# RWKV attention into a SwiGLU FFN: grouping the FFN by batches at the start, with a new order of all steps

## The chip, the cores and the metric

The kernel runs on one core of a Trainium2 chip. The metric is the device time of one execution in microseconds. A core has five instruction queues that run independently: TensorE (PE: matmuls, transposes by matmul, and its weight loads, PEld), VectorE (DVE), ScalarE (ACT), GpSimd (POOL) and SyncE (SP, which issues most transfers). Each runs its own instructions in order and waits on semaphores for the others. Matmuls write to PSUM, eight banks of 2 KB per partition; everything else lies in SBUF or in HBM.

## The reference

Four batches, 8 heads, 768 time steps, head width 48. A linear recurrence with decay w feeds an RMS norm and a gated FFN (384 to 1536 to 384):

```
for t in range(S):
    cur = einsum('bhd,bhe->bhde', u * k_t, v_t)
    y_t = einsum('bhd,bhde->bhe', r_t, state + cur)
    state = w_t[..., None] * state + einsum('bhd,bhe->bhde', k_t, v_t)
x  = y as (B*S, 384)
xn = x / sqrt(mean(x*x) + 1e-6) * rms_g
out = (silu(xn @ w_gate) * (xn @ w_val)) @ w_out
```

## The kernel before

The 768 steps are cut into 6 chunks of 128 (n = 0 to 5). A unit is one chunk of one batch (j = 0 to 3), so there are 24 attention units, and a batch's chunk n + 1 needs the state of its chunk n. The FFN runs once per chunk, over the four batches' 4 x 128 = 512 tokens: 12 blocks f of 128 hidden features.

The order of all work is written out by hand in ORDER (L25 to L128), a list of steps `name.n.j`; the loop at L691 calls the function of that name, which appends instructions to the engines' queues. So the place of a step in ORDER is its place in each queue it uses.

For an attention unit the steps are: load_w, load_r, load_k, load_v (SP; in chunks 0 and 1 one load_w brings both chunks of a batch); ln (ACT, log of w); cs_mm (PE, cumulative sums), cs_add (DVE, chunks 2 to 5); exp_r and exp_k (ACT); r_mul (DVE) and k_mul (DVE or POOL, by K_POOL); w_tot (DVE); rk_pe with rk_tr (PE transposes and a copy out of PSUM, chunks 0 and 1) or rk_tr alone (a transposing transfer); q_mm (PE), q_mask_e (DVE), q_copy_o (ACT) with q_mask_o (POOL), or q_mask_o on DVE; bonus_mul (POOL: r times k, then times u), bonus_sum (DVE), bonus_v (POOL); cast_v (ACT or POOL, by CAST_ACT); y_mm (PE); st_mm (PE) and st_new (DVE) for the state; x_pe (PE) or x_add (DVE); x_sq (ACT), x_rstd (ACT or POOL, by RSTD_ACT), xn_mul (ACT); xn_pe with xn_out (PE, DVE), or xn_tr with xn_gain (transfer, then DVE or ACT) in the last two chunks.

For the FFN of a chunk: gate_mm and val_mm (PE, three matmuls each, fc_mm at L626), silu (ACT), h_mul (DVE, L658) for each f, then o_mm (PE, twelve matmuls, L672), o_out (DVE or ACT, by OUT_DVE) and out_dma (SP) for each batch. The last o_mm is split into two halves of 192 columns.

PSUM is handed out by psum() from three rings: "a" (two banks: gate, cumulative sums, some y), "b" (two banks: val, cumulative sums, some y) and "q" (four banks: the rest). act() loads ScalarE's table at L233 whenever a step needs Exp or Ln behind Silu or the reverse. The FFN weights come by load_gv(g, h) and load_wo(g) on POOL's queue, cast from fp32 to bf16 on the way; gate and val are cut at f = 0, 4, 12, so there are four such loads of unequal size, and three for w_out. 13 dummy matmuls at L285 and 36 warm steps (L374) on zeros keep PE busy at the start.

The kernel's text with its line numbers, cut to what the change touches:

Of the kernel before, what the change touches and what calls it, by code (L numbers as in the profile page):

```python
# [25 lines left out]
load_w.0.1 load_r.0.0 load_w.0.0 warm.4.0 warm.18.0 load_r.0.1 load_k.0.1 load_w.0.2 load_k.0.0 ln.0.1 load_k.0.2  # L26
load_w.0.3 ln.0.0 load_r.0.2 warm.31.0 load_v.0.0 load_v.0.1 warm.22.0 load_k.0.3 load_r.0.3 load_v.0.3 load_v.0.2
cs_mm.0.1 exp_r.0.1 exp_k.0.1 cs_mm.0.0 load_r.1.1 load_k.1.0 load_r.1.0 load_k.1.1 w_tot.0.1 ln.0.2 warm.10.0
load_r.1.3 load_k.1.3 load_r.1.2 load_k.1.2 r_mul.0.1 load_v.1.0 load_v.1.2 load_v.1.1 exp_k.0.0 bonus_mul.0.1
load_v.1.3 load_w.2.0 warm.7.0 exp_r.0.0 k_mul.0.1 bonus_mul.0.0 rk_pe.0.1 w_tot.0.0 warm.2.0 warm.21.0 load_w.2.1  # L30
rk_tr.0.1 warm.9.0 cs_mm.0.2 warm.27.0 bonus_sum.0.1 exp_r.0.2 r_mul.0.0 k_mul.0.0 bonus_mul.0.2 warm.12.0 warm.34.0
warm.13.0 ln.0.3 r_mul.0.2 warm.26.0 rk_pe.0.0 exp_k.0.2 warm.5.0 rk_tr.0.0 load_r.2.1 load_w.2.2 warm.19.0 warm.32.0
cast_v.0.0 cs_mm.0.3 load_r.2.0 load_k.2.0 q_mm.0.1 warm.8.0 w_tot.0.2 k_mul.0.2 bonus_sum.0.0 exp_k.0.3 cs_mm.1.0
bonus_v.0.1 q_mm.0.0 exp_r.0.3 exp_k.1.0 q_mask_e.0.1 q_mask_o.0.1 bonus_sum.0.2 k_mul.0.3 exp_r.1.0 w_tot.0.3
r_mul.0.3 warm.24.0 warm.29.0 rk_pe.0.2 warm.1.0 x_pe.0.1 cast_v.0.1 rk_tr.0.2 y_mm.0.1 bonus_v.0.0 bonus_mul.0.3
q_mask_o.0.0 rk_pe.0.3 q_mask_e.0.0 q_mm.0.2 x_pe.0.0 x_sq.0.1 cast_v.0.3 rk_tr.0.3 bonus_sum.0.3 q_mask_o.0.2
load_gv.0.0 q_mask_e.0.2 cs_mm.1.1 x_rstd.0.1 q_mm.0.3 warm.17.0 bonus_v.0.2 q_mask_o.0.3 y_mm.0.0 warm.25.0 exp_r.1.1
load_w.2.3 x_pe.0.2 load_k.2.1 cast_v.0.2 bonus_v.0.3 warm.20.0 x_sq.0.0 y_mm.0.2 st_mm.0.0 warm.6.0 warm.35.0
xn_mul.0.1 x_rstd.0.0 x_sq.0.2 warm.15.0 q_mask_e.0.3 warm.23.0 x_pe.0.3 xn_mul.0.0 warm.3.0 warm.16.0 y_mm.0.3
exp_k.1.1 cs_mm.1.3 k_mul.1.0 xn_pe.0.1 warm.0.0 bonus_mul.1.0 load_gv.0.1 load_gv.1.0 x_rstd.0.2 warm.30.0 x_sq.0.3  # L40
xn_mul.0.2 r_mul.1.0 st_new.0.0 xn_pe.0.0 warm.14.0 x_rstd.0.3 warm.28.0 warm.33.0 xn_pe.0.2 xn_out.0.1 bonus_mul.1.1
warm.11.0 xn_mul.0.3 exp_k.1.3 xn_out.0.0 st_mm.0.3 xn_out.0.2 st_mm.0.2 xn_pe.0.3 exp_r.1.3 cs_mm.1.2 xn_out.0.3
r_mul.1.1 st_new.0.3 k_mul.1.1 k_mul.1.3 gate_mm.0.0 exp_r.1.2 bonus_sum.1.0 exp_k.1.2 gate_mm.0.3 st_mm.0.1
st_new.0.1 rk_pe.1.0 val_mm.0.0 rk_pe.1.1 silu.0.0 rk_tr.1.0 bonus_sum.1.1 load_gv.1.1 load_r.2.2 bonus_mul.1.3
silu.0.3 val_mm.0.2 rk_tr.1.1 h_mul.0.0 gate_mm.0.2 st_new.0.2 silu.0.2 gate_mm.0.1 bonus_sum.1.3 val_mm.0.3
gate_mm.0.9 silu.0.1 h_mul.0.2 val_mm.0.1 gate_mm.0.6 silu.0.9 r_mul.1.3 h_mul.0.3 q_mm.1.0 h_mul.0.1 silu.0.6
q_mask_e.1.0 q_copy_o.1.0 q_mask_o.1.0 gate_mm.0.11 gate_mm.0.7 q_copy_o.1.1 silu.0.7 rk_pe.1.3 q_mask_e.1.1
q_mask_o.1.1 r_mul.1.2 bonus_v.1.0 val_mm.0.6 val_mm.0.7 k_mul.1.2 rk_tr.1.3 cast_v.1.0 gate_mm.0.5 h_mul.0.6 y_mm.1.0
load_wo.0.0 val_mm.0.9 silu.0.11 bonus_v.1.1 cast_v.1.2 load_wo.1.0 st_mm.1.0 cast_v.1.1 gate_mm.0.4 rk_pe.1.2
h_mul.0.7 st_mm.1.1 silu.0.5 val_mm.0.5 x_add.1.0 rk_tr.1.2 h_mul.0.9 cast_v.1.3 gate_mm.0.10 bonus_mul.1.2 val_mm.0.4  # L50
st_new.1.0 st_new.1.1 load_wo.2.0 q_mm.1.2 h_mul.0.5 silu.0.4 x_sq.1.0 h_mul.0.4 gate_mm.0.8 bonus_v.1.3 q_copy_o.1.3
x_rstd.1.0 q_mask_e.1.3 q_copy_o.1.2 val_mm.0.8 silu.0.8 val_mm.0.11 y_mm.1.1 silu.0.10 q_mask_e.1.2 bonus_sum.1.2
q_mask_o.1.3 h_mul.0.8 x_add.1.1 y_mm.1.3 st_mm.1.2 load_v.2.1 ln.2.0 st_mm.1.3 q_mask_o.1.2 val_mm.0.10 y_mm.1.2
x_sq.1.1 xn_mul.1.0 bonus_v.1.2 cs_mm.2.0 x_add.1.3 x_sq.1.3 st_new.1.2 h_mul.0.11 ln.2.1 h_mul.0.10 x_add.1.2
cs_add.2.0 o_mm.0.0 o_out.0.0 x_rstd.1.1 x_sq.1.2 xn_pe.1.0 xn_out.1.0 xn_mul.1.1 exp_r.2.0 st_new.1.3 cs_mm.2.1
cs_add.2.1 x_rstd.1.2 load_r.2.3 r_mul.2.0 o_mm.0.2 xn_pe.1.1 xn_mul.1.2 xn_pe.1.2 x_rstd.1.3 o_mm.0.1 xn_mul.1.3
bonus_mul.2.0 xn_out.1.1 exp_k.2.0 out_dma.0.0 load_k.2.2 exp_r.2.1 w_tot.2.0 load_v.2.0 ln.2.2 k_mul.2.0 ln.2.3
w_tot.2.1 r_mul.2.1 cs_mm.2.2 xn_pe.1.3 cs_mm.2.3 exp_k.2.1 xn_out.1.2 cs_add.2.2 k_mul.2.1 cs_add.2.3 cast_v.2.1
exp_r.2.2 exp_r.2.3 rk_tr.2.1 xn_out.1.3 o_mm.0.3 exp_k.2.3 o_out.0.1 w_tot.2.2 r_mul.2.2 bonus_mul.2.1 gate_mm.1.7
val_mm.1.7 exp_k.2.2 load_k.2.3 st_mm.2.1 rk_tr.2.0 bonus_sum.2.0 r_mul.2.3 w_tot.2.3 gate_mm.1.1 load_v.2.2  # L60
# [664 lines left out]
```

## Time and profile before

| quantity | value |
|---|---|
| median of 3 runs | 200.59 us (200.36 to 200.87) |
| span of the profiled execution | 199.6 us |
| busy in that span: PE, DVE, ACT, POOL | 192.4, 151.6, 137.5, 125.0 us |
| weight loads (PEld) | 113.9 us |
| granted TensorE clock, mean | 0.999 |
| HBM read, written | 25.96 MB, 4.72 MB |

The profiled execution's span reaches from its first to its last instruction. Rows of the profile name a line of the kernel, the engine, the operation, output <- input by the program's names, the shape, and a count; then busy time, the mean of one in ns, and the idle time of the engine just before such instructions with what ended it. PE's busy time counts the dummy matmuls too, and the ends of matmuls are modelled, so that start to start is the better measure of one.

### The profile page before, as it was taken

What the parts mean: (1) busy time and instruction counts of PE and PEld (TensorE: products, weight loads), DVE (VectorE), ACT (ScalarE), POOL (GpSimd) and SP (SyncE); (2) the same over time, 40 slices, a digit from 0 to 9 for tenths busy, and PEclk for the clock granted to TensorE, in tenths of its full rate; (3) what the DMA queues carried; (4) which work ended last, traced back from release to release, by engine and by line L of the source; (5) the groups of instructions that cost most, each with busy time, mean ns of one, the idle gap of its engine ahead of it and who ended that gap; (6) DMA issues with size and microseconds to landing.
All of it is one profiled execution on the core that took longest, in us unless ns stands there. A gap on an engine that the chain in (4) does not pass through costs nothing.

```text
span 199.6 us, 4410 instructions
## 1 busy us (share of the span) xinstructions
PE 192.4 (96%) x1577; PEld 113.9 (57%) x1577; DVE 151.6 (76%) x290; ACT 137.5 (69%) x279; POOL 125.0 (63%) x184
## 2 busy tenths in 40 slices
...
GB/s 148 249 230 174 184 194 204 201 207 198 156 180 233 181 158 235 226 205 204 208 213 220 211 197 207 171 176 148 116 181 232 1 23 61 0 118 82 0 59 100
DMA packets 121566, 32.41 MB, mean 162 GB/s; under 512 B 116420, under 2 KB 120392, under 8 KB 121544
## 3 DMA queue, kind: packets, MB, share of 16 engines
...
q0 software_dynamic: 2032, 3.54, 10.1%
q8 instruction: 12, 0.20, 0.4%
q14 instruction: 10, 0.08, 0.1%
...
HBM read 25.96 MB, written 4.72 MB: 154 GB/s over the span
## 4 chain that ended last, share of the span: by engine, by line
PE 71%; SPq 13%; DMA 11%; POOL 2%; issue 1%; ACT 0%; POOLq 0%
SPq L248 11%; PE ps_av L626 10%; PE ps_bu L626 10%; PE ps_bv L626 10%; PE ps_au L626 9%; DMA vt<-in_v_dram 7%; PE ps_qz L672 7%; PE ps_qv L672 7%; PE ps_qu L672 5%; PE ps_qx L672 4%; DMA wo_sb<-in_moe_w_out_dram 4%; SPq L261 2%; PE ps_qv L502 1%; PE ps_qx L552 1%; PE ps_av L417 1%
## 5 line engine op out<-in xcount | busy, mean ns | idle before, releaser
L672 PEld LDWEIGHTS <-ht 128*128 128x128 bf16 x300 | 28.2, 98 | 17.3 <-issue 0.7
L626 PEld LDWEIGHTS <-wg_sb 128*128 128x128 bf16 x216 | 23.1, 114 | 20.2 <-DMA wg_sb<-in_moe_w_gate_dram 0.7
L626 PEld LDWEIGHTS <-wv_sb 128*128 128x128 bf16 x216 | 22.8, 114 | 18.6 <-DMA wv_sb<-in_moe_w_val_dram 0.5
L658 DVE TENSOR_TENSOR ht<-ps_bv,sg 128x512 bf16<-128x512 f32 x35 | 24.0, 686 | 10.1 <-PE ps_bv L626 9.2
L235 ACT ACTIVATE sg<-ps_av 128x512 bf16<-128x512 f32 x37 | 22.0, 595 | 12.3 <-PE ps_av L626 12.1
L626 PE MATMUL ps_av<-xnt,wg_sb 128*128 128x512 bf16 x111 | 30.1, 380 | 0.0
L626 PE MATMUL ps_bu<-xnt,wv_sb 128*128 128x512 bf16 x111 | 30.1, 380 | 0.0
L658 DVE TENSOR_TENSOR ht<-ps_bu,sg 128x512 bf16<-128x512 f32 x37 | 25.4, 686 | 6.0 <-PE ps_bu L626 5.2
L467 POOL TENSOR_TENSOR ruk<-rt,kt 128x384 f32<-128x384 f32 x24 | 24.0, 1002 | 8.7 <-DVE wcol L446 4.5
L626 PE MATMUL ps_bv<-xnt,wv_sb 128*128 128x512 bf16 x105 | 28.5, 380 | 0.3 <-DMA wv_sb<-in_moe_w_val_dram 0.3
L626 PE MATMUL ps_au<-xnt,wg_sb 128*128 128x512 bf16 x105 | 28.5, 380 | 0.3 <-DMA wg_sb<-in_moe_w_gate_dram 0.2
L235 ACT ACTIVATE sg<-ps_au 128x512 bf16<-128x512 f32 x35 | 21.0, 599 | 10.8 <-PE ps_au L626 9.0
L468 POOL TENSOR_TENSOR ruk<-ruk,u_bc 128x384 f32<-128x384 f32 x24 | 24.4, 1017 | 1.9
L520 POOL TENSOR_SCALAR_AFFINE_SELECT qts<-qts 128x512 bf16<-128x512 bf16 x20 | 12.8, 649 | 13.8 <-ACT qts L513 13.2
L477 POOL TENSOR_TENSOR ydiag<-vt,diag 128x384 f32<-128x384 f32 x24 | 19.8, 831 | 1.2 <-DMA vt<-in_v_dram 0.7
L461 POOL TENSOR_TENSOR rk<-kt,ek 128x384 bf16<-128x384 f32 x16 | 15.9, 1007 | 2.5 <-ACT ek L235 2.3
L235 ACT ACTIVATE lw<-wt 128x384 bf16<-128x384 f32 (+1 forms) x20 | 11.2, 580 | 5.6 <-DMA wt<-in_w_dram 5.5
L672 PE MATMUL ps_qz<-wo_sb,ht 128*128 128x384 bf16 (+1 forms) x96 | 15.0, 306 | 0.0
L672 PE MATMUL ps_qv<-wo_sb,ht 128*128 128x384 bf16 x84 | 14.8, 326 | 0.0
L233 ACT ACT_TABLE_LOAD x10 | 12.8, 1283 | 1.8 <-PEq L709 1.6
L472 DVE TENSOR_REDUCE diag<-ruk 128x8 f32<-128x384 f32 x24 | 13.0, 544 | 0.6 <-POOL ruk L468 0.5
L585 ACT ACTIVATE xn<-xb,rstd 128x384 bf16<-128x384 f32 x20 | 11.8, 605 | 0.8 <-POOL rstd L580 0.7
...
## 6 DMA issues: line engine op xcount, KB each, us to landing
...
wt<-in_w_dram SPq DMA_DIRECT2D x4, 384.0 KB, 4.6
wo_sb<-in_moe_w_out_dram POOLq DMA_DIRECT2D x3, 384.0 KB, 7.2
wg_sb<-in_moe_w_gate_dram POOLq DMA_DIRECT2D x1, 768.0 KB, 9.8
```

Of the source, the lines that this page charges most:

```text
L233: nc.scalar.preload_act_table_set(table_name)
L235: return nc.scalar.activation(**kw).ins
L248: dmas["load_" + which, n, j] = nc.sync.dma_start(out=inp[which, n, j], in_=t[j, :, n * L:(n + 1) * L, :].rearrange("h t d -> t h d")).ins
L461: eng.tensor_tensor(out=rk[:, n % 2, j, 1, :, 0:D], in0=inp["k", n, j], in1=bank["cs_k", n, j][:, 0:DM].rearrange("p (h d) -> p h d", h=H) ...
L467: nc.gpsimd.tensor_tensor(out=ruk[n, j], in0=inp["r", n, j], in1=inp["k", n, j], op=ALU.mult)
L468: nc.gpsimd.tensor_tensor(out=ruk[n, j], in0=ruk[n, j], in1=u_bc, op=ALU.mult)
L472: nc.vector.tensor_reduce(out=diag[n, j].rearrange("p h o -> p (h o)"), in_=ruk[n, j], axis=mybir.AxisListType.X, op=ALU.add)
L477: nc.gpsimd.tensor_tensor(out=ydiag[n, j], in0=inp["v", n, j], in1=diag[n, j].to_broadcast([128, H, D]), op=ALU.mult)
L520: nc.gpsimd.affine_select(out=qts[n, j][:, 1], in_=qts[n, j][:, 1], compare_op=ALU.is_gt, fill=0.0, base=0, pattern=[[0, NP], [1, 128]], c ...
L626: nc.tensor.matmul(ps[:, cols], lhsT=units(ws, c, f), rhs=xnt[n][:, c, cols], start=(first and c == 0), stop=(c == KC - 1))
L658: nc.vector.tensor_tensor(out=ht[n][:, f, :], in0=bank.pop(("v", n, f)), in1=bank.pop(("sg", n, f)), op=ALU.mult)
L672: nc.tensor.matmul(ps[:, cols], lhsT=ht[n][:, f, b * L:(b + 1) * L], rhs=wo_sb[:, f, cols], start=(f == 0), stop=(f == FC - 1))
```

## The change

GROUPS replaces "one FFN per chunk". A group is a list of (chunk, batch) units whose tokens form one FFN pass, and steps of the FFN are now numbered by group: group 0 is batches 0 and 1 with chunks 0 and 1 (512 tokens), group 1 is batch 2 and group 2 is batch 3, each with chunks 0 and 1 (two units, 256 tokens), and groups 3 to 6 are chunks 2 to 5 with all four batches. The tuples are (chunk, batch), as out_dma unpacks them.

gate_mm, val_mm, silu and h_mul work on as many columns as the group has; there are 84 of each instead of 72. The gate and val weights are cut at f = 0, 4, 8, 12, so load_gv runs six times with equal sizes. A first product of bonus_mul stays on POOL, the second moves to DVE (bonus_u, reading u from PSUM) for the four units of BU_DVE; two xn_mul move to DVE (XNM_DVE). The sets that choose engines for casts, k_mul, copies, evictions and the rest are new; rk_tr of four units moves to DVE. warm steps fall from 36 to 16. The factor 1/384 of the mean is folded into gT as a square root, and options that were not in use are gone. ORDER is written anew from beginning to end; it begins and, around the first gates and group 1, goes on as shown.

```diff
--- before
+++ after
+load_w.0.1 load_w.0.0 load_k.0.0 ln.0.0 load_r.0.0 load_r.1.0 ln.0.1 warm.0.0 cs_mm.0.0 exp_r.0.0 cs_mm.1.0 exp_k.0.0
+exp_r.1.0 k_mul.0.0 r_mul.1.0 exp_k.1.0 load_k.1.0 w_tot.0.0 load_r.0.1 r_mul.0.0 bonus_mul.0.0 load_k.0.1 load_r.1.1
+load_v.0.0 warm.1.0 warm.2.0 warm.3.0 warm.4.0 cs_mm.0.1 rk_pe.0.0 k_mul.1.0 exp_r.0.1 bonus_u.0.0 bonus_mul.1.0
+rk_pe.1.0 exp_k.0.1 rk_tr.0.0 load_k.1.1 cs_mm.1.1 exp_r.1.1 r_mul.0.1 bonus_sum.0.0 bonus_u.1.0 warm.5.0 warm.6.0
+warm.7.0 q_mm.0.0 bonus_sum.1.0 exp_k.1.1 k_mul.0.1 load_w.0.2 load_v.0.1 load_w.0.3 bonus_mul.0.1 load_v.1.0
+q_mask_e.0.0 load_v.1.1 load_r.0.2 load_k.0.2 warm.14.0 warm.15.0 rk_pe.0.1 load_w.2.0 load_k.1.2 rk_tr.1.0 w_tot.0.1
...
+y_mm.1.0 w_tot.0.2 q_mask_e.1.1 warm.21.0 warm.22.0 x_pe.1.1 x_sq.1.0 x_rstd.1.0 xn_mul.0.1 k_mul.0.2 r_mul.0.2
+xn_pe.0.0 y_mm.1.1 x_sq.1.1 xn_mul.1.0 xn_pe.0.1 x_rstd.1.1 load_k.1.3 load_w.2.1 load_gv.0.0 xn_out.0.1 bonus_mul.0.2
+warm.23.0 warm.24.0 rk_pe.0.2 load_k.0.3 xn_mul.1.1 xn_pe.1.0 load_gv.1.0 cs_mm.1.3 xn_pe.1.1 ln.2.0 xn_out.0.0
+exp_k.1.3 exp_r.1.3 xn_out.1.0 cs_mm.1.2 rk_tr.0.2 xn_out.1.1 q_mm.0.2 exp_k.1.2 load_r.0.3 exp_r.1.2 load_r.2.0
+gate_mm.0.9 q_mask_e.0.2 silu.0.9 st_mm.1.1 st_mm.1.0 gate_mm.0.11 st_new.1.1 val_mm.0.9 silu.0.11 val_mm.0.11
+bonus_sum.0.2 gate_mm.0.10 load_gv.1.1 h_mul.0.9 load_gv.0.1 bonus_v.0.2 q_copy_o.0.2 h_mul.0.11 silu.0.10
+q_mask_o.0.2 val_mm.0.10 gate_mm.0.1 h_mul.0.10 st_new.1.0 silu.0.1 gate_mm.0.8 val_mm.0.8 cast_v.0.2 gate_mm.0.5
...
+load_wo.2.0 load_k.2.3 load_w.3.3 bonus_mul.0.3 gate_mm.1.5 gate_mm.1.7 q_copy_o.1.3 val_mm.1.2 silu.1.5 silu.1.7
+val_mm.1.8 bonus_sum.1.3 st_new.0.3 gate_mm.1.8 h_mul.1.2 silu.1.8 gate_mm.1.6 q_mask_o.1.3 q_mask_e.1.3 q_mm.0.3
...
+xn_tr.5.3 xn_tr.5.2 xn_gain.6.0 h_mul.5.11 xn_gain.6.2 xn_gain.6.1 o_mm.5.2 o_mm.5.3 gate_mm.6.2 gate_mm.6.8
...
+    GROUPS = (
+        ((0, 0), (1, 0), (0, 1), (1, 1)),
+        ((0, 2), (1, 2)),
+        ((0, 3), (1, 3)),
+        ((2, 0), (2, 1), (2, 2), (2, 3)),
+        ((3, 0), (3, 1), (3, 2), (3, 3)),
+        ((4, 0), (4, 1), (4, 2), (4, 3)),
+        ((5, 0), (5, 1), (5, 2), (5, 3)),
+    )
+    place = {unit: (g, c) for g, units_of in enumerate(GROUPS) for c, unit in enumerate(units_of)}
+    NG = len(GROUPS)
...
-    CAST_ACT = sel("00 01 02 03 10 11 12 13")
-    EXPR_SB = sel("10 11 12 13")
-    K_POOL = sel("20 21 22 23 30 31 32 33 40 41 42 43 50 51 52 53")
+    CAST_ACT = sel("03 10 11 12 21 30 40 41 42 52")
+    EXPR_SB = sel("02 03 12 13")
+    EXPK_SB = sel("02 03 12 13 20 21 22 23 30 31 32 33 40 41 42 43 50 51 52 53")
+    K_POOL = sel("02 03 13 20 21 22 30 31 32 40 41 42 43 50 51 53")
+    RK_DVE = sel("02 03 12 13")
+    ODD_DVE = sel("00 01 10 11")
+    RSTD_ACT = sel("01 03 10 11 13 42 43")
+    X_PE = sel("00 01 10 11")
+    BU_DVE = sel("00 01 10 11")
+    XNM_DVE = sel("01 10")
+    GAIN_ACT = sel("52 62")
+    GAIN_POOL = sel("50 60")
+    OUT_DVE = sel("02 31 41 50 60 63")
+    GV = (0, 4, 8, 12)
-    OUT_DVE = sel("00 02 10 12 20 22 30 32 40 42 50 52 53")
...
     def bonus_mul(n, j):
         ruk[n, j] = pt.tile([128, H, D], FP32, name="ruk", bufs=NRUK)
         nc.gpsimd.tensor_tensor(out=ruk[n, j], in0=inp["r", n, j], in1=inp["k", n, j], op=ALU.mult)
-        nc.gpsimd.tensor_tensor(out=ruk[n, j], in0=ruk[n, j], in1=u_bc, op=ALU.mult)
+        if (n, j) not in BU_DVE:
+            nc.gpsimd.tensor_tensor(out=ruk[n, j], in0=ruk[n, j], in1=u_bc, op=ALU.mult)
+
+    def bonus_u(n, j):
+        nc.vector.tensor_tensor(out=ruk[n, j], in0=u_ps.rearrange("p (h d) -> p h d", h=H), in1=ruk[n, j], op=ALU.mult)
...
+    def xn_cols(n, j):
+        g, c = place[n, j]
+        if g not in xnt:
+            xnt[g] = pt.tile([128, KC, TS], BF16, name="xnt")
+        return xnt[g][:, :, c * L:(c + 1) * L]
...
+    def fc_mm(ps, ws, n, f):
         for c in range(KC):
-            nc.tensor.matmul(ps[:, cols], lhsT=units(ws, c, f), rhs=xnt[n][:, c, cols],
-                             start=(first and c == 0), stop=(c == KC - 1))
+            nc.tensor.matmul(ps, lhsT=units(ws, c, f), rhs=xnt[n][:, c, 0:cols_of(n)],
+                             start=(c == 0), stop=(c == KC - 1))
...
     def out_dma(n, j):
-        b, cols = out_cols(n, j)
-        row0 = b * S + n * L
+        c, cols = out_cols(n, j)
+        chunk, b = GROUPS[n][c]
+        row0 = b * S + chunk * L
```

320 lines of the change are left out of this document (131 added, 189 removed).

## The prediction

> **What bounds the kernel now.** I read the windows first, cut at the first FFN matmul (29.75), at the end of the last PE wait for a transfer (54.10) and at FFN boundaries. Columns: the stretch, its length, busy microseconds (instructions) of PE, PEld, DVE, ACT, POOL, the granted clock, the DMA share, GB/s.
>
> ```profile
> 29.75:54.10 24.35, 23.28 (x217) 13.84 (x218) 23.34 (x40) 19.70 (x36) 13.76 (x20) 1.00 1.07 198
> 54.10:82.00 27.90, 27.89 (x244) 16.61 (x244) 24.67 (x49) 21.68 (x44) 22.51 (x33) 1.00 1.01 193
> 138.60:165.50 26.90, 26.90 (x209) 15.53 (x207) 21.52 (x39) 20.94 (x46) 19.14 (x30) 1.00 0.48 103
> ```
>
> From 54 on PE has no gap, while DVE has about 3 us spare per 28. Then I read PE's timeline for its start, its waits and its end (start, duration, instruction, idle time before it).
>
> ```profile
> 29.75 0.81 PE L626 MATMUL ps_au<-xnt,wg_sb 128*128 128x512 bf16 x3
> 30.40 0.81 PE L626 MATMUL ps_av<-xnt,wg_sb 128*128 128x512 bf16 x3
> ...
> 32.17 0.84 PE L626 MATMUL ps_bv<-xnt,wv_sb 128*128 128x512 bf16 x3 [0.34 <-DMA wv_sb<-in_moe_w_val_dram]
> ...
> 36.40 0.84 PE L626 MATMUL ps_au<-xnt,wg_sb 128*128 128x512 bf16 x3 [0.22 <-DMA wg_sb<-in_moe_w_gate_dram]
> ...
> 54.11 0.81 PE L672 MATMUL ps_qx<-wo_sb,ht 128*128 128x384 bf16 x4 [0.52 <-DMA wo_sb<-in_moe_w_out_dram]
> ...
> 196.71 0.32 ACT L681 COPY ob<-ps_qz 128x192 f32<-128x192 f32 x1 [2.46 <-PE ps_qz L672]
> ```
>
> So the span of 199.6 is 29.75 until FFN work starts, 166.96 from there to PE's end (196.71), and 2.9 for the last eviction and store. Of the 166.96, 1.08 (0.34 + 0.22 + 0.52) is waiting for weights; 165.9 is work. The median of the runs, 200.59, lies 1.0 above the span; I carry that 1.0 along. Only three things can change the time: when the first gate_mm starts, how much PE work is left then, and PE's waits.
>
> **PE work: unchanged.** The reading above fixes the gate matmul: three instructions each 0.65 after the last (30.40 - 29.75). The new list has 84 gate and 84 val steps instead of 72, but 48 of them are 256 columns wide, so the columns are the same. Whether a narrow matmul pays for its weight load shows in the 128-column transposes of rk_pe:
>
> ```profile
> 44.58 0.61 PE L484 MATMUL ps_qu<-ident,rk 128*128 128x128 bf16 x8
> 45.02 0.33 PE L530 MATMUL ps_qz<-vb,rk 128*128 128x96 bf16 x4
> ```
>
> Eight with eight weight loads take 0.44, 55 ns each; a quarter of a 512-column matmul (0.65/3 = 217 ns) is 54. At 256 columns I take 0.33 for three, so the split costs PE about 24 x 2 x 0.33 - 24 x 0.65 = 0.2; the bounds are 0 and 0.3. All other PE steps but warm occur equally often. Ahead of the first gate the new list has one rk_pe and one q_mm more, one cs_mm and one st_mm less, and two y_mm of chunk 1 in place of chunk 0: the difference is near 0. The 20 dropped warm steps are not on the path later. So 165.9 stays 166.
>
> **First gate: earlier.** Its last input is now xn_out.1.1 (chunk 1, batch 1), where it was xn_out.0.3. Three floors bear on it.
>
> ```profile
> 8.14 0.54 DVE L455 TENSOR_TENSOR rk<-rt,ps_au 128x384 bf16<-128x384 f32 x1
> 8.60 0.55 DVE L461 TENSOR_TENSOR rk<-kt,ps_bu 128x384 bf16<-128x384 f32 x1
> ...
> 15.71 0.69 DVE L509 TENSOR_TENSOR qts<-ps_qv,mask_lt 128x512 bf16<-128x512 f32 x1
> 16.32 0.68 DVE L517 TENSOR_TENSOR qts<-ps_qz,mask_lt 128x512 bf16<-128x512 f32 x1
> ...
> 29.05 0.56 DVE L607 TENSOR_TENSOR xnt<-ps_qv,gT 128x384 bf16<-128x384 bf16 x1 [0.20 <-PE ps_qv L596]
> ```
> ```profile
> 18.86 0.99 POOL L467 TENSOR_TENSOR ruk<-rt,kt 128x384 f32<-128x384 f32 x1 [1.03 <-DMA rt<-in_r_dram]
> ```
> ```profile
> L455 DVE TENSOR_TENSOR rk<-rt,er 128x384 bf16<-128x384 f32 x4 | 4.6, 1149 | 0.0
> ```
>
> DVE: back to back a 384-wide step costs 0.46 (8.60 - 8.14) and a 512-wide mask 0.61. Up to xn_out.1.1 the new list gives DVE 24 steps of the first kind (k_mul 4, r_mul 4, bonus_u 4, bonus_sum 4, st_new 2, xn_mul 2, xn_out 4: 11.0), eight masks (4.9), r_mul.0.2 with both operands in SBUF (1.1), three small w_tot (0.3) and rk_tr.0.2, a 1024-wide copy not in the trace. From 0.46 and 0.61 it extrapolates to 0.46 + 5 x 0.15 = 1.2; below, 0.61 if it ran at twice the rate. I take 1.2, because xn_out, also bf16 out of PSUM, runs at the full 0.56. Sum 18.5, and from 8.1 the floor is 26.6. The same sum for before is 15.5, but there xn_out.0.3 ended at 29.6, so DVE waited 6 of 21.5.
>
> The Trainium skill, VectorE: DVE Perf Modes (The perf-mode tier table), allows a copy out of PSUM up to twice the rate; by it the copy would be some 0.6, the floor 26.0, and the time 0.6 less. No row here shows it.
>
> Data: the load of r.0.3 was the 18th unit of 192 KB (a w load is two) and landed at 18.8, so one unit takes 1.04. The new list has v.1.1 as 20th unit: 20.9. Behind it come bonus_v, x_pe, y_mm, x_sq, x_rstd, xn_mul, xn_pe, xn_out, about 5: 26. ACT: up to the last xn_mul it loses two casts, two xn_mul and one x_rstd, about 2.4 of what kept it full in the 20s. DVE is the latest floor; I add 0.9 for waits that remain and take 27.5. Gain 29.75 - 27.5 = 2.25; bounds 3.1 (no waits) and 0 (waits as before).
>
> **Weights: six loads instead of four.**
>
> ```profile
> 20.87 0.99 POOL L351 DMA_DIRECT2D wg_sb<-in_moe_w_gate_dram  x1
> ...
> 29.32 0.80 POOL L351 DMA_DIRECT2D wv_sb<-in_moe_w_val_dram  x1
> ```
> ```profile
> wo_sb<-in_moe_w_out_dram POOLq DMA_DIRECT2D x3, 384.0 KB, 7.2
> ...
> wv_sb<-in_moe_w_val_dram POOLq DMA_DIRECT2D x1, 768.0 KB, 11.3
> wg_sb<-in_moe_w_gate_dram POOLq DMA_DIRECT2D x1, 384.0 KB, 6.2
> ```
> ```profile
> 27.52 14.01 SPq L248 DMA_DIRECT2D vt<-in_v_dram  x4
> ```
>
> The last of them landed at 29.32 + 11.3 = 40.6. In the new list POOL issues behind bonus_v.1.0, bonus_v.1.1, k_mul.0.2 and bonus_mul.0.2: about 20.7, 22.5, 24.3, 27.1, 27.9, 28.7, the same bytes with the last as late as before. So I keep 40.6 for the sixth, 6.2 behind the issue for the first two (26.9, 28.7), and even steps between: 31.7, 34.7, 37.6. PE walks: val.0.9 at 29.2 and gate.0.1 at 31.8 wait for nothing, gate.0.5 (33.8) waits 0.9, val.0.5 (37.0) 0.6, val.0.1 (39.8) 0.8. Sum 2.3; bounds 0.5 (as before) and 4. wo is first read by o_mm.0.2, behind 27 us of the new list's PE work (27.5 + 27 + 2.3 = 57). POOL issues it behind k_mul.0.3, which waits for ACT's Exp phase ahead of the 20 us mark of that work, so near 48; it lands 7 to 8 later, with no wait. Net waits: 2.3 - 1.08 = +1.2. Meanwhile SP's loads starve, as the four v loads above did for 14 us; batch 3's come some 42 to 46, before rk_pe.1.3 and rk_pe.0.3 in the list.
>
> **What lies beside PE.** More ACT work:
>
> ```profile
> L233 ACT ACT_TABLE_LOAD x10 | 12.8, 1283 | 1.8 <-PEq L709 1.6
> L235 ACT ACTIVATE sg<-ps_av 128x512 bf16<-128x512 f32 x37 | 22.0, 595 | 12.3 <-PE ps_av L626 12.1
> L235 ACT ACTIVATE ek<-ps_bv 128x384 f32<-128x384 f32 x10 | 4.8, 484 | 0.0
> L658 DVE TENSOR_TENSOR ht<-ps_bv,sg 128x512 bf16<-128x512 f32 x35 | 24.0, 686 | 10.1 <-PE ps_bv L626 9.2
> ```
> ```profile
> 30.27 1.28 ACT L233 ACT_TABLE_LOAD   x1
> 31.56 0.60 ACT L235 ACTIVATE sg<-ps_au 128x512 bf16<-128x512 f32 x1
> ```
>
> Counting Exp/Ln against Silu along the list gives 12 table loads instead of 10: 2.6. Seven more evictions (about 0.48 each) are ACT's, 3.4; twelve more silus, at 256 columns 0.37 (484 less the 111 that 128 columns cost), add 1.3 to 1.7; DVE's h_mul at 0.42 likewise, less seven evictions, plus three rk_tr. Behind the first gate ACT gains about 7 and DVE 2 against PE's 166: hidden by PE at 27.9 of 27.9, taken as 0. Folding the square root of 384 into gT and dropping unused options (all None) changes no instruction on the path. The Trainium skill, ScalarE: Activation LUTs (What ACT_TABLE_LOAD costs), adds a drain of about 1.38 to each switch; by it the two cost 5.3. The rows disagree: the silu starts 0.01 behind the load.
>
> The last FFN loses cover: two o_mm instead of four stand between the last attention and its gates.
>
> ```profile
> 161.89 0.36 PE L552 MATMUL ps_qx<-vb,qts 128*128 128x48 bf16 x8
> 164.21 0.55 DVE L561 TENSOR_TENSOR xb<-ps_qx,ydiag 128x384 f32<-128x384 f32 x1
> 169.49 0.88 DVE L615 TENSOR_SCALAR xnt<-xnt,gT 128x512 bf16<-128x512 bf16 x3 [2.81 <-DMA xnt<-xn]
> ```
>
> From the last y_mm (162.2) to the gains' end (170.4) it took 8.2, of which x_add stood 2.0 in DVE's queue. The new list has five gate/val steps and two o_mm there, 7.1, and x_add at once: 6.2 to 8.2, so 0; bound 1.1.
>
> Sum: 200.59 - 2.25 + 1.2 = **199.5**.
>
> **Rivals.** (C) slower: in groups 1 and 2 PE is tied to DVE.
>
> ```profile
> 187.39 0.81 PE L626 MATMUL ps_av<-xnt,wg_sb 128*128 128x512 bf16 x3
> 188.23 0.60 ACT L235 ACTIVATE sg<-ps_av 128x512 bf16<-128x512 f32 x1 [1.35 <-PE ps_av L626]
> 188.95 0.69 DVE L658 TENSOR_TENSOR ht<-ps_bu,sg 128x512 bf16<-128x512 f32 x1 [0.60 <-PE ps_bu L626]
> ```
>
> From the gate's end (188.04) to h_mul's end is 1.6; at half width 1.1. The two val banks give PE four narrow steps, 1.3, until it needs that bank. It decides as soon as more than 0.2 of other work stands ahead on ACT or DVE; one 0.55 step in every second pair makes 12 x 0.3 = 3.6: 203.1. Against it: attention steps stand between those gates and lengthen the 1.3. (D) the first gate doesn't come earlier, because DVE keeps its 6 us of waits behind loads and has 3 more to do: 200.59 + 1.2 = 201.8. (B) the weights come in time and DVE has no waits: 200.59 - 3.1 - 1.1 + 0.3 = 196.7. (E) with 16 warm steps for 36, PE's clock falls.
>
> ```profile
> 1.34 0.53 PE L285 MATMUL ps_qv<-still 128*128 128x384 bf16 x1
> 1.66 0.53 PE L285 MATMUL ps_qx<-still 128*128 128x384 bf16 x1
> ...
> 8.54 0.32 PE L374 MATMUL ps_qz<-still 128*128 128x384 bf16 x1
> 8.70 0.33 PE L374 MATMUL ps_qu<-still 128*128 128x384 bf16 x1
> ```
>
> A dummy takes 0.32 at first and 0.16 from the fifth microsecond on, so about 3.3 us of work ran at half rate. The same once more at the first gates loses 1.6: 201.1. The Trainium skill, TensorE: Matmul & The Clock Gate (What's actually happening), has the clock halve after an idle window of some 3.4 us; I find no such gap in the new list, so little weight.
>
> **How the numbers follow.** Forecast 0.42 (own range 198.0 to 200.6), B 0.18, C 0.22, D 0.10, E 0.08. A measurement here tells 0.3%, 0.6 us, from no change: under 199.99 is faster, over 201.19 slower. Seven tenths of the forecast (0.30) and B: faster 0.48. The rest of it and E: 0.20. C and D: slower 0.32. The range reaches from B to C, 196.5 to 203.2.
>
> **What would show it.** Right: the first L626 matmul at 26.6 to 28; waits of L626 on wg_sb and wv_sb of about 2 in 33 to 41; PE full from 58 on. Wrong: the first gate past 29; L626 waiting on ACT's sg or DVE's ht between 45 and 75 (C); the granted clock under 1 before 31 (E); PE idle ahead of the last FFN's gates.

## The result, and the profile after

The changed kernel takes 207.81 us (median of 4 runs, 206.83 to 209.59) where the kernel before takes 200.73 beside it: 1.0355 times as long, 95% interval 1.0292 to 1.0418. That is slower, and above the predicted range. Ratios, here and below, leave out executions over 1.5% longer than the fastest of the same kernel; medians keep them. The profiled execution is the fastest of the four, 206.83 with a span of 205.1, so its rows show about 5.5 us of the 7.

PE's timeline after, the rows that answer to those of the prediction (start, duration, instruction, idle time before it with what ended it):

```profile
25.75 0.61 PE L489 MATMUL ps_qv<-ident,rk 128*128 128x128 bf16 x8 [1.17 <-DVE xnt L608]
28.33 0.81 PE L627 MATMUL ps_au<-xnt,wg_sb 128*128 128x512 bf16 x2
...
30.54 0.84 PE L627 MATMUL ps_bv<-xnt,wv_sb 128*128 128x512 bf16 x3 [0.41 <-DMA wv_sb<-in_moe_w_val_dram]
35.51 0.84 PE L627 MATMUL ps_av<-xnt,wg_sb 128*128 128x512 bf16 x3 [0.25 <-DMA wg_sb<-in_moe_w_gate_dram]
37.96 0.84 PE L627 MATMUL ps_bv<-xnt,wv_sb 128*128 128x512 bf16 x3 [0.32 <-DMA wv_sb<-in_moe_w_val_dram]
...
47.51 0.32 PE L418 MATMUL ps_av<-lw,mask_lt 128*128 128x384 bf16 x1 [0.86 <-ACT er L251]
48.56 0.84 PE L627 MATMUL ps_au<-xnt,wg_sb 128*128 128x512 bf16 x2 [0.32 <-DVE wcol L452]
...
51.79 0.49 PE L627 MATMUL ps_av<-xnt,wg_sb 128*128 128x256 bf16 x3
52.12 0.49 PE L627 MATMUL ps_bu<-xnt,wv_sb 128*128 128x256 bf16 x3
...
93.46 0.84 PE L627 MATMUL ps_au<-xnt,wg_sb 128*128 128x512 bf16 x3 [0.62 <-DVE wcol L452]
117.36 0.32 PE L418 MATMUL ps_au<-lw,mask_lt 128*128 128x384 bf16 x1 [0.46 <-DVE rk L456]
124.98 0.23 PE L507 MATMUL ps_qx<-rkT 48*128 48x128 bf16 x1 [0.20 <-DMA rkT<-rk]
141.02 0.35 PE L557 MATMUL ps_qz<-vb,qts 128*128 128x48 bf16 x7 [0.19 <-POOL qts L525]
146.40 0.32 PE L418 MATMUL ps_au<-lw,mask_lt 128*128 128x384 bf16 x1 [0.30 <-DVE rk L456]
151.22 0.81 PE L627 MATMUL ps_au<-xnt,wg_sb 128*128 128x512 bf16 x2 [0.44 <-POOL xnt L616]
174.34 0.81 PE L627 MATMUL ps_av<-xnt,wg_sb 128*128 128x512 bf16 x3 [0.64 <-POOL xnt L616]
```

The start is better in this execution: the first gate_mm stands at 28.33, not 29.75. The weights are no worse: 0.41 + 0.25 + 0.32 = 0.98 against 1.08. The new cost is in the rows below them. At 47.5 PE waits for ACT and DVE (0.86 + 0.32), and from 93 on there are seven waits, 2.85 together, on DVE, a transfer and POOL in turn. The kernel before has no wait of PE behind 54.11. Where that goes is seen in the windows, first before, then after (columns as in the prediction):

```profile
92.00:120.00 28.00, 28.00 (x246) 16.82 (x245) 25.16 (x50) 20.81 (x44) 23.32 (x35) 1.00 1.04 208
120.00:148.00 28.00, 28.00 (x224) 16.36 (x223) 23.93 (x45) 22.37 (x47) 22.16 (x32) 1.00 0.82 165
148.00:173.00 25.00, 25.00 (x196) 14.39 (x195) 15.30 (x28) 14.38 (x30) 13.15 (x23) 1.00 0.33 77
```
```profile
50.00:80.00 30.00, 30.00 (x314) 24.23 (x312) 26.88 (x60) 23.59 (x57) 23.26 (x30) 1.00 1.04 198
...
92.00:120.00 28.00, 26.69 (x237) 15.84 (x237) 24.03 (x48) 22.77 (x48) 19.83 (x29) 1.00 1.05 198
120.00:148.00 28.00, 27.10 (x214) 15.68 (x216) 22.60 (x43) 22.20 (x48) 18.93 (x26) 1.00 0.81 174
148.00:176.00 28.00, 26.70 (x198) 15.20 (x200) 17.84 (x32) 19.35 (x41) 19.33 (x27) 1.00 0.33 84
```

From 50 to 80, where the narrow groups 1 and 2 run, PE is full. From 92 to 176, where each FFN is one chunk of four batches in both kernels, it is idle 1.31 + 0.90 + 1.30 = 3.5 us, and the clock is 1.00 throughout. So most of the time is not lost where the FFN is grouped anew. The first gate_mm of the first four-batch FFN says the same: it stands at 91.21, and at 90.75 before. From its gain of 1.42 the change has fallen 0.5 behind by there; the other 5.0 of the 5.5 are lost behind it. ACT has 64.3 us to do in those three rows (84 us), against 57.6 in before's three (81 us). The chain of work that ended last, read by engine, lies less on PE: before, PE had 71% of it and POOL 2%; now

```profile
PE 45%; POOL 18%; DMA 14%; ACT 9%; issue 6%; DVE 5%; POOLq 1%; SPq 1%; ACTq 0%; DVEq 0%
```

The account of the two profiled executions: the first gate -1.42; annotated waits between it and 92, 2.16 against 1.08, +1.08; those behind 92, +2.85; each wait, twelve instead of three, keeps PE from its next matmul some 0.16 longer than annotated (taken from the starts: 1.02 for the 0.86 at 47.51), +1.4; the tail behind PE's last work, 3.3 for 2.9, +0.4. That is 4.3 of the 5.5; some 1.2 is not placed. Gaps too short to be annotated add up to 1.0 in the changed kernel, but most of them are 0.05 long and stand where the record of one matmul is missing (x2 for x3 in the row of 28.33: the next start is 0.43 later, two matmuls of 0.22).

```profile
201.81 0.36 DVE L667 COPY ob<-ps_qu 128x192 f32<-128x192 f32 x1 [5.32 <-PE ps_qu L660]
```

The better start does not come in every execution. Fourteen traces of this case have this list up to the first gate. In ten of them it stands at 28.06 to 28.60; in four (the runs below with the gains on DVE, the earlier loads, less POOL and no stores) at 30.06 to 30.08, later than before's 29.75. PE's first cumulative sums tell them apart. In the changed kernel's profile they start 0.33 after one another, in the run with the gains on DVE 0.64:

```profile
7.34 0.49 PE L403 MATMUL ps_av<-lw,mw 128*128 128x384 bf16 x2
7.67 0.49 PE L410 MATMUL ps_bv<-lw,mw 128*128 128x384 bf16 x2
```
```profile
8.89 0.84 PE L403 MATMUL ps_av<-lw,mw 128*128 128x384 bf16 x2
9.53 0.84 PE L410 MATMUL ps_bv<-lw,mw 128*128 128x384 bf16 x2
...
30.06 0.81 PE L627 MATMUL ps_au<-xnt,wg_sb 128*128 128x512 bf16 x2
```

In the four, PE's matmuls run at half rate until 10 us, in the ten only until 4 to 6. The kernel before's list has the long half rate too, in one of four traces (the run with more work in chunk 2); there the first gate stands at 29.31, no later than in the other three (29.48 to 29.75). How often it comes in executions without a trace is not known.

### The profile page after: what moved, and what is told of

The parts are those of the page before. It is cut to its first block, busy times and chain, and to the rows that moved or that the text cites. A ratio compares the mean times of both kernels' runs of the same rounds, so it can differ in the third digit from the quotient of the medians.

```text
span 205.1 us, 4537 instructions
## 1 busy us (share of the span) xinstructions
PE 191.1 (93%) x1614; PEld 120.2 (59%) x1629; DVE 153.2 (75%) x302; ACT 142.4 (69%) x303; POOL 123.9 (60%) x176
## 4 chain that ended last, share of the span: by engine, by line
PE 45%; POOL 18%; DMA 14%; ACT 9%; issue 6%; DVE 5%; POOLq 1%; SPq 1%; ACTq 0%; DVEq 0%
PE ps_av L627 7%; PE ps_au L627 6%; PE ps_bv L627 6%; PE ps_bu L627 6%; DMA wv_sb<-in_moe_w_val_dram 5%; PE ps_qz L660 5%; PE ps_qv L660 4%; POOL rk L462 3%; POOL ruk L468 3%; POOL ruk L470 2%; PE ps_qu L660 2%; DMA vt<-in_v_dram 2%; DMA kt<-in_k_dram 2%; POOL ydiag L482 2%; ACT junk L571 2%
## 5 line engine op out<-in xcount | busy, mean ns | idle before, releaser
L645 DVE TENSOR_TENSOR ht<-ps_bu,sg 128x512 bf16<-128x512 f32 (+1 forms) x42 | 25.9, 616 | 11.7 <-PE ps_bu L627 6.6
L645 DVE TENSOR_TENSOR ht<-ps_bv,sg 128x512 bf16<-128x512 f32 (+1 forms) x42 | 25.3, 603 | 12.0 <-PE ps_bv L627 6.2
L627 PE MATMUL ps_au<-xnt,wg_sb 128*128 128x512 bf16 (+1 forms) x125 | 30.8, 349 | 1.7 <-DVE wcol L452 0.9
L251 ACT ACTIVATE sg<-ps_av 128x512 bf16<-128x512 f32 (+1 forms) x41 | 21.9, 535 | 14.3 <-PE ps_av L627 8.6
L627 PE MATMUL ps_bv<-xnt,wv_sb 128*128 128x512 bf16 (+1 forms) x124 | 29.9, 347 | 0.8 <-DMA wv_sb<-in_moe_w_val_dram 0.7
L627 PE MATMUL ps_av<-xnt,wg_sb 128*128 128x512 bf16 (+1 forms) x119 | 29.2, 348 | 1.2 <-POOL xnt L616 0.6
L251 ACT ACTIVATE sg<-ps_au 128x512 bf16<-128x512 f32 (+1 forms) x43 | 23.1, 538 | 9.8 <-PE ps_au L627 5.5
L627 PE MATMUL ps_bu<-xnt,wv_sb 128*128 128x512 bf16 (+1 forms) x121 | 29.7, 350 | 0.1
L660 PE MATMUL ps_qz<-wo_sb,ht 128*128 128x384 bf16 x108 | 19.0, 326 | 0.0
L571 ACT ACTIVATE junk<-xb 128x384 bf16<-128x384 f32 x20 | 10.3, 517 | 3.9 <-DVE xb L566 3.7
```

Of the source, the lines that this page charges most:

```text
L251: return nc.scalar.activation(**kw).ins
L571: nc.scalar.activation(out=junk, in_=xb[n, j], func=AF.Square, accum_out=rstd[n, j][:, 0:1])
L627: nc.tensor.matmul(ps, lhsT=units(ws, c, f), rhs=xnt[n][:, c, 0:cols_of(n)], start=(c == 0), stop=(c == KC - 1))
L645: nc.vector.tensor_tensor(out=ht[n][:, f, 0:cols_of(n)], in0=bank.pop(("v", n, f)), in1=bank.pop(("sg", n, f)), op=ALU.mult)
L660: nc.tensor.matmul(ps[:, cols], lhsT=ht[n][:, f, b * L:(b + 1) * L], rhs=wo_sb[:, f, cols], start=(f == 0), stop=(f == FC - 1))
```

## The experiments

Ratios are to the kernel before, run beside each; the whole change stands at 1.0355 [1.0292, 1.0418]. Theories at the start: the loss is made in chunks 3 to 5 by the new order (with POOL and late loads as its carrier), or the new start leaves a debt.

### Laced orders

Before's order from the groups' end on, behind the new start, and the mirror; the two lists were laced by cumulative PE work.

```diff
-warm.4.0 cs_mm.0.1 rk_pe.0.0 k_mul.1.0
+warm.4.0 cs_mm.0.1 load_w.2.0 load_w.2.1 rk_pe.0.0 k_mul.1.0
```

> The changed kernel with its new groups, its new list and its engine choices for chunks 0 and 1 and FFN groups 0 to 2, but with the old order and the old engine choices for chunks 2 to 5 and their FFNs (the two lists laced together by TensorE work). Theory A, the loss sits in the new order and choices of chunks 2 to 5: about 200, between 198.5 and 202. Rival B, the loss comes from the groups at the start (their transfers and DVE work push everything behind them): 205 to 208.

> The mirror image: the kernel before with its own chunks 0 and 1 (one FFN per chunk, four batches each), and from chunk 2 on the new order and the new engine choices. Theory A: 204 to 208, most of the loss is there without any groups. Rival B: 199.5 to 201.5.

Measured: 246.52, ratio 1.2282 [1.222, 1.2344], and 248.44, ratio 1.2366 [1.2276, 1.2455], at a mean clock of 0.930 and 0.938. Both cost 46 us or more, far outside either theory, so they test neither. Only PE's work was laced evenly, the other four queues' was not; that this is the reason is not shown.

### The gains of xnt, and earlier loads

```diff
-    GAIN_POOL = sel("50 60")
+    GAIN_POOL = sel("")
```

> The changed kernel with the two xn_gain steps that run on POOL put back on DVE, nothing else. In the changed kernel's trace such a step takes 1.73 us on POOL and 0.35 on DVE, and TensorE waits 0.44 and 0.64 for it at the last two FFN starts. If those waits are on the path: 1.2 to 1.6 less than the changed kernel's 207.8, so 206.2 to 206.6. Rival, the transposing transfers or ACT's own gain step end just as late: 207.3 or more.

Measured: 207.56, ratio 1.0362 [1.0291, 1.0434], no gain. POOL takes 1.73 for a gain that DVE does in 0.35 and ACT in 0.72 (the gains of the last FFN; POOL's and then DVE's timeline of the changed kernel):

```profile
172.56 1.73 POOL L616 TENSOR_SCALAR xnt<-xnt,gT 128x512 bf16<-128x512 bf16 x1 [3.76 <-DMA xnt<-xn]
```
```profile
172.49 0.35 DVE L616 TENSOR_SCALAR xnt<-xnt,gT 128x512 bf16<-128x512 bf16 x1 [1.89 <-DMA xnt<-xn]
```

Moved to DVE, the gain at 151 stands behind what DVE still has to do, and the one at 174 waits 2.55 for its transfer and holds up an h_mul behind it. PE's waits of that run:

```profile
152.53 0.84 PE L627 MATMUL ps_au<-xnt,wg_sb 128*128 128x512 bf16 x2 [1.41 <-DVE xnt L616]
174.86 0.34 PE L660 MATMUL ps_qx<-wo_sb,ht 128*128 128x384 bf16 x1 [1.93 <-DVE ht L645]
```

The waits for POOL (0.44 and 0.64) became waits of 1.41 and 1.93. So the wait row names the last arrival, not what is worth removing.

For the loads of chunks 3 to 5, each was put 8 us of PE work earlier in the list, for instance

```diff
-rk_tr.4.0 load_v.4.1 r_mul.4.3 load_v.5.2 gate_mm.4.9
+x_sq.3.2 o_mm.3.0 load_v.4.1 load_v.5.2 load_r.5.2
```

> The changed kernel with every load of chunks 3 to 5 moved ahead in the list by 8 us of TensorE work, nothing else. If the late loads (POOL waits 7.7 us for v, ACT and DVE for w and r between 100 and 180) are what makes TensorE stall at the starts of chunks 3 to 5: 2 to 4 less, 204 to 206. Rival, these waits lie beside TensorE's work and the stalls come from the order of the DVE and ACT steps: 207 to 208.5.

Measured: 222.58, ratio 1.1079 [1.1015, 1.1142]. SP's own waits in that run (in all, times, longest):

```profile
SPq L674 <- ACT ob L667: 31.9, 6, 10.8
SPq L492 <- POOL ruk L466: 14.1, 6, 9.1
```

The transposes of rk (L492, L494 in the changed kernel) now wait 14.1 us for POOL's bonus_mul. In the changed kernel it was

```profile
SPq L494 <- POOL ruk L468: 5.7, 4, 3.4
```

On an in-order queue, moving loads moves everything behind them too. The edit is no clean test of "loads too late", and no gain.

### Spliced orders

The two lists differ in only 18 of 701 steps done at one place, the first gate_mm of the first four-batch FFN (91 us). There they were cut and joined, with the engine choices of each part.

```diff
-ln.4.0 xn_out.2.2 bonus_mul.3.0 o_mm.2.1 gate_mm.3.1 k_mul.3.0 k_mul.3.3 val_mm.3.11
+ln.4.0 xn_out.2.2 bonus_mul.3.0 o_mm.2.1 gate_mm.3.5 val_mm.3.0 k_mul.3.0 bonus_mul.3.2
...
-    CAST_ACT = sel("03 10 11 12 21 30 40 41 42 52")
+    CAST_ACT = sel("03 10 11 12 21")
```

> The new kernel's own list of steps up to the first gate_mm of its first four-batch FFN (91.2 us in its trace), and from there the list of before from the same place (90.9 us in its trace), with before's choice of engines for chunks 3 to 5 and the last four FFNs. The two lists are joined where the sets of steps already done differ in only 18 of 701, so nothing is laced. Theory 'the loss is in the new order of chunks 3 to 5': the second half takes what it took before, so the time is 200.6 + 0.3 (the lag of the first gate there) + 0 to 2 for the seam = 201 to 203. Rival 'the new start leaves engines and buffers behind, and the debt comes due later': 205 to 208, as the whole change.

> The mirror: before's list up to the same place (its gate_mm.2.5 at 90.9 us), and from there the new list, with the new choice of engines for chunks 3 to 5. Theory 'the loss is in the new order of chunks 3 to 5': 205 to 208, that is 200.6 plus the 5 us lost between 92 and 176 plus 0 to 2 for the seam. Rival 'the new start leaves a debt': 199.5 to 202.

Measured: 206.17, ratio 1.0299 [1.0268, 1.0329], and 209.35, ratio 1.0476 [1.0423, 1.0528]. The first looks like the rival, but PE's waits behind 92 in its profile are two, both at the seam:

```profile
93.97 0.81 PE L625 MATMUL ps_av<-xnt,wg_sb 128*128 128x512 bf16 x3 [1.86 <-ACT sg L249]
...
98.25 0.21 PE L507 MATMUL ps_qz<-rkT 48*128 48x128 bf16 x1 [1.59 <-ACT ob L667]
```

Behind 99, before's second half runs without an annotated wait. Either ACT arrived late at 92 (a debt) or the join itself made it late. The mirror pays 0.68 to 2.90 a wait at its seam too. The seams cost as much as was to be told apart, so both runs are inconclusive.

### The engine choices, and the stores

The new order with before's choices for chunks 3 to 5 and the last FFNs; then the output stores issued by ACT.

```diff
-    CAST_ACT = sel("03 10 11 12 21 30 40 41 42 52")
-    K_POOL = sel("02 03 13 20 21 22 30 31 32 40 41 42 43 50 51 53")
-    RSTD_ACT = sel("01 03 10 11 13 42 43")
-    GAIN_ACT = sel("52 62")
-    GAIN_POOL = sel("50 60")
-    OUT_DVE = sel("02 31 41 50 60 63")
+    CAST_ACT = sel("03 10 11 12 21")
+    K_POOL = sel("02 03 13 20 21 22 30 31 32 33 40 41 42 43 50 51 52 53")
+    RSTD_ACT = sel("01 03 10 11 13")
+    GAIN_ACT = sel("51")
+    GAIN_POOL = sel("")
+    OUT_DVE = sel("02 30 32 40 42 50 52 60 62 63")
```

> The new order unchanged, but before's choice of engines for chunks 3 to 5 and the last four FFNs: five casts and two rstd back from ACT to POOL, two k_mul from DVE to POOL, the gains of POOL to DVE, the output evictions shared between DVE and ACT as before. Theory 'POOL with its late loads is the chain in the new order': POOL gets about 7 us more to do and the time rises to 209 to 213. Rival 'it is ACT, which does 7 us more from 92 on than before': 203 to 205. If order alone decides and the choices are fitted to neither: 206.5 to 208.5.

```diff
-        nc.sync.dma_start(out=out[row0:row0 + L, cols], in_=bank.pop(("ob", n, j))[:, cols])
+        nc.scalar.dma_start(out=out[row0:row0 + L, cols], in_=bank.pop(("ob", n, j))[:, cols])
```

> The new kernel with only the output stores issued by ACT instead of SP, so a store that waits for its eviction (27 us of SP's waiting, longest 10.8) no longer holds up loads and transposes behind it. Theory 'SP's in-order queue makes loads late': 203.5 to 206, as far as the issue on ACT (28 stores) does not take it back. Rival 'the loads are late because of where they stand behind the transposes, or do not matter': 207 to 209.

Measured: 210.65, ratio 1.0525 [1.0468, 1.0582], and 215.13, ratio 1.0647 [1.0556, 1.0738]. The first says that the new choices, six sets changed together, suit this order better than before's, by 3.4 us; it does not part them. It agrees with the POOL theory, but its largest waits are DVE's (PE's waits, in all, times, longest):

```profile
PE ps_qx L660 <- DVE ht L645: 1.9, 1, 1.9
PE ps_av L418 <- DVE rk L456: 1.4, 1, 1.4
PE ps_au L627 <- DVE xnt L616: 1.4, 1, 1.4
```

In the second the stall moved: PE waited 3.8 and 1.9 for evictions (ob, L669) that now stand among ACT's stores. It does not show what SP's waits cost.

### Work taken away, engine by engine

To avoid moving anything, work was left out in place: POOL's second bonus product, ACT's squares, DVE's sums and state additions, all in chunks 3 to 5; then the stores of groups 2 to 5.

```diff
-        if (n, j) not in BU_DVE:
+        if (n, j) not in BU_DVE and n < 3:
```

> The new kernel without the second product of the bonus (by u, POOL, 1.0 us each, 12 of them) in chunks 3 to 5, so the outputs lack that factor there. Nothing else moves. Theory 'POOL is what PE's partners wait for in chunks 3 to 5' (18% of the chain that ended last, before 2%): 3 to 4 of the 5 us lost there come back, 203.5 to 205. Rivals 'ACT' or 'DVE': 206.5 to 208, since POOL had idle time. Rival 'fixed places in the lists decide, not the amount of work': 206.5 to 208 here and in the next two runs.

```diff
-        nc.scalar.activation(out=junk, in_=xb[n, j], func=AF.Square, accum_out=rstd[n, j][:, 0:1])
+        if n < 3 or (n, j) in RSTD_ACT:
+            nc.scalar.activation(out=junk, in_=xb[n, j], func=AF.Square, accum_out=rstd[n, j][:, 0:1])
...
+                nc.gpsimd.tensor_scalar(out=ss, in0=xb[n, j][:, 0:1], scalar1=1.0, scalar2=None, op0=ALU.max)
```

> The new kernel without ten of the twelve squares of chunks 3 to 5 (ACT, 0.52 + 0.19 us each, 7 us in all); POOL's rstd reads a column of its input instead, so the normalisation there is by a wrong factor. Theory POOL: 206 to 208 (the path to xn becomes 0.7 us shorter, which may help POOL a little). Rival 'ACT, which has 7 us more to do between 92 and 176 than in the kernel before': 203 to 205. Rival 'places': 206.5 to 208.

```diff
-        nc.vector.tensor_reduce(out=diag[n, j].rearrange("p h o -> p (h o)"), in_=ruk[n, j],
+        w = D if n < 3 else D // 8
+        nc.vector.tensor_reduce(out=diag[n, j].rearrange("p h o -> p (h o)"), in_=ruk[n, j][:, :, 0:w],
...
-        if n in OLD_DVE:
+        if n in OLD_DVE and n < 3:
```

> The new kernel with the bonus sums of chunks 3 to 5 over an eighth of the columns (DVE, 0.54 us each, 12) and without the addition of the old state in st_new of chunks 3 and 4 (0.56 us each, 8 of them): some 8 us of DVE less, outputs wrong there. Theory POOL: 206.5 to 208. Rival 'DVE is the one that PE waits for' (it has the same 64 us to do between 92 and 176 as before, and was the busiest engine beside PE): 203 to 205. Rival 'places': 206.5 to 208.

```diff
+        if n in (2, 3, 4, 5):
+            bank.pop(("ob", n, j))
+            return
         nc.sync.dma_start(out=out[row0:row0 + L, cols], in_=bank.pop(("ob", n, j))[:, cols])
```

> The new kernel without the output stores of groups 2 to 5 (the outputs of those groups stay unwritten); the evictions stay. SP no longer waits for an eviction (27 us in all, longest 10.8), and loads and transposes behind a store go out when their own inputs allow. Theory 'SP's in-order queue makes loads and transposes late': 203 to 205.5. Rival 'what SP waits for at the stores costs nothing': 207 to 208.5.

| less | median us | ratio | 95% interval |
|---|---|---|---|
| POOL | 205.64 | 1.0230 | 1.0162 to 1.0298 |
| ACT | 204.38 | 1.0201 | 1.0140 to 1.0262 |
| DVE | 205.28 | 1.0240 | 1.0194 to 1.0286 |
| stores | 206.01 | 1.0266 | 1.0204 to 1.0328 |

The POOL theory falls: 12 us less on POOL give back (1.0355 - 1.0230) x 200.6 = 2.5, and 7 or 8 us less on ACT or DVE as much, 3.1 and 2.3. "Places" alone falls too, since work counts. ACT's and DVE's intervals lie clear of that of the whole change, POOL's touches it. The stores are unclear: theirs overlaps it.

The late first gate blurs this table, since POOL's and the stores' profiled executions have it (30.08 and 30.07) and the other two do not. From the first gate to PE's end, in one execution each, the changed kernel takes 173.4 us, without POOL's work 171.2, without ACT's 170.4, without DVE's 171.3 and without the stores 170.8 (before: 166.9). By that measure the stores count as much as the engines. Leaving out the squares also takes a step of 0.7 out of the path to xn, and no run took away work that should not matter, so these runs do not say which engine's load is the cause.

### Ahead of 92 or behind it, and all at once

The same three reliefs, in chunk 2 alone, in chunk 3 alone, and in chunks 3 to 5 together (the edits above with n in (2,), (3,) or (3, 4, 5)).

> The new kernel with the reliefs of e9, e10 and e11 together, but in chunk 2 alone, whose steps lie ahead of 92 us: POOL 4 us less, ACT 2.8, DVE 3.9 (no bonus product by u, no squares, sums over an eighth of the columns, no addition of the old state; outputs of chunk 2 wrong). Theory 'the new order of chunks 3 to 5 itself leaves no cover': what is saved ahead of 92 is used up there, 206.5 to 208. Rival 'the new start leaves its engines behind at 92, and the debt is paid in chunks 3 to 5': 203 to 205.5.

> The same reliefs in chunk 3 alone (some 90 to 120 us): POOL 4 us less, ACT 2.8, DVE 3.9. Theory 'order of chunks 3 to 5': about a third of what chunks 3 to 5 give together, 205 to 206.5, with the waits at 146 to 174 still there. Rival 'debt': the debt of 92 is paid here, 203 to 204.5, and the waits at 146 to 174 shrink.

> The new kernel with the three reliefs of e9, e10 and e11 together in chunks 3 to 5 (POOL 12 us less, ACT 7, DVE 8). Alone they gave back 2.4, 3.1 and 2.3 us by the ratios. Theory 'all partners at once, none with cover': they add up until PE is full, 200 to 202. Rival 'a fixed part sits in places of the list (the waits of 117, 150 and 173 us, which stood in all three runs)': no better than the best of them less 1, 203 to 204.5.

Measured: chunk 2, 204.46, ratio 1.0209 [1.0168, 1.0249]; chunk 3, 204.51, ratio 1.0224 [1.0155, 1.0293]; all, 204.76, ratio 1.0240 [1.0176, 1.0305]. Relief ahead of 92 is worth as much as relief behind it, some 3 us, which my theory had excluded. The run with relief in chunk 2, its windows behind 92 and its waits of PE from 28 on:

```profile
92.00:120.00 28.00, 27.79 (x246) 16.88 (x248) 25.45 (x52) 23.05 (x51) 21.28 (x30) 1.00 1.08 207
120.00:148.00 28.00, 27.25 (x212) 15.83 (x215) 23.52 (x43) 22.90 (x49) 20.14 (x26) 1.00 0.80 166
148.00:176.00 28.00, 27.16 (x196) 15.29 (x199) 15.55 (x27) 18.57 (x38) 15.81 (x24) 1.00 0.28 72
```
```profile
PE ps_av L418 <- ACT er L251: 0.9, 1, 0.9
PE ps_av L632 <- POOL xnt L621: 0.6, 1, 0.6
...
PE ps_au L632 <- POOL xnt L621: 0.4, 1, 0.4
```

Of the seven waits behind 92 five are gone (93, 117, 125, 141 and 146 us); PE's idle time there falls from 3.5 to 1.8, and in those chunks nothing was edited (of the edited steps only the last state addition stands behind 92 in the list). PE comes to the first gate there 0.9 sooner (90.28 for 91.21) and from it to its end takes 107.9 us instead of 110.6. So ACT, DVE and POOL come to 92 too late, and the lag shows up to 54 us later. What stays are the weights, the waits at chunk 2's entry (0.86 at 47) and the two waits for POOL's gains.

All at once gave no more than one alone. Nearly 5 us (1.024 x 200.6 = 205.4 against 200.6) are not to be had by taking work off these engines in chunks 3 to 5.

### The same from the other side

The kernel before with the product r*k, the square and the bonus sum of chunk 2 done twice:

```diff
         nc.gpsimd.tensor_tensor(out=ruk[n, j], in0=inp["r", n, j], in1=inp["k", n, j], op=ALU.mult)
+        if n == 2:
+            nc.gpsimd.tensor_tensor(out=ruk[n, j], in0=inp["r", n, j], in1=inp["k", n, j], op=ALU.mult)
```

> The kernel before with a debt of that kind made on purpose: in chunk 2 the product r*k (POOL, 1.0 us, 4), the square (ACT, 0.7 us, 4) and the bonus sum (DVE, 0.54 us, 4) are done twice, with the same output. Theory 'order of chunks 3 to 5': the old order takes it up in its idle time, 200.3 to 201.5. Rival 'debt': 202 to 204.5, with new PE waits from 92 us on.

Measured: 204.0, ratio 1.0182 [1.0138, 1.0225]. PE's waits in its profiled execution (205.11):

```profile
PE ps_bu L633 <- DVE ht L665: 1.3, 1, 1.3
PE ps_bv L633 <- DMA wv_sb<-in_moe_w_val_dram: 1.3, 1, 1.3
PE ps_au L633 <- DMA wg_sb<-in_moe_w_gate_dram: 1.0, 1, 1.0
PE ps_qz L603 <- ACT xn L592: 0.8, 1, 0.8
```

So before has no idle time to take up 4 us of POOL, 2.8 of ACT and 2.2 of DVE in chunk 2. Two reservations: the weight waits of 1.3 and 1.0 lie at 33 and 38 us, ahead of the edit, in an execution with the half rate until 10 us, and the rest stand between 68 and 90, none behind 92 as the rival had it.

### The two table loads

The change gives ACT 12 table loads instead of 10. The last two runs take two out of the new kernel (those at 50.3 and 58.8; ten silus between them become exponentials of the same size) and put two into the kernel before.

```diff
+        if (n, f) in ((0, 6), (1, 3), (1, 2), (1, 5), (1, 7), (1, 8), (1, 6), (1, 1), (1, 9), (1, 0)):
+            act(LN_EXP, out=sg, in_=bank.pop(("g", n, f)), func=AF.Exp, scale=-1.0)
+            return
         act(SILU, out=sg, in_=bank.pop(("g", n, f)), func=AF.Silu)
```

> The new kernel with the ten silus between the table loads of 50.3 and 58.8 us replaced by exponentials of the same size, which the table already loaded serves; both loads go, 2.57 us of ACT, all else stays (ten of the 36 FFN steps of the first three groups get a wrong function). Theory 'the two more loads are the debt at 92': 204.5 to 206, some 2 to 3 us back, and the waits of 93 and 117 us shrink. Rival 'the debt is of the rest of the new start': 207 to 208.5.

```diff
     def exp_r(n, j):
+        if (n, j) == (2, 2):
+            nc.scalar.preload_act_table_set(SILU)
+            nc.scalar.preload_act_table_set(LN_EXP)
```

> The kernel before with two table loads more, back to back in the middle of chunk 2's exponentials (between 50 and 62.7 us), with the same output. Theory 'two loads are a debt': 201.5 to 203.5, with PE waits between 60 and 95 us that the kernel before does not have. Rival: 200 to 200.9, taken up by ACT's idle time (2.8 us of it ahead of silus between 44 and 92).

Measured: 205.21, ratio 1.0264 [1.0221, 1.0306], so 1.8 us back (the intervals just overlap); and 201.71, ratio 1.0081 [1.0053, 1.0110], so 1.6 us lost, 1.1 to 2.2. In the second the cost has a place. ACT's timeline and then PE's:

```profile
58.86 1.28 ACT L431 ACT_TABLE_LOAD   x1
60.15 1.28 ACT L432 ACT_TABLE_LOAD   x1
61.45 0.48 ACT L235 ACTIVATE ps_au<-ps_au 128x388 f32<-128x388 f32 x1
```
```profile
62.64 0.84 PE L629 MATMUL ps_au<-xnt,wg_sb 128*128 128x512 bf16 x2 [1.28 <-DVE rk L458]
```

The exponential starts 1.8 after its input from DVE is there (59.07 + 0.57; ACT would have waited 0.8 for it in any case), DVE's r_mul after it, and the gate that needs the same bank of ring "a" after that: half of the loads' 2.57 us reaches PE as 1.28. The loads behave as in the prediction's rows, with no drain behind them (58.86 + 1.28 ends 0.01 ahead of 60.15), so the row held against the 1.38 that the Trainium skill, ScalarE: Activation LUTs (What ACT_TABLE_LOAD costs), adds.

## Why the prediction was wrong, by its steps

**What lies beside PE: the step that failed.** It counted ACT's work rightly, 12 table loads among it (behind the first gate ACT is busy 123.3 us, 115.5 before; DVE has 1.2 less, not 2 more), and then set it to nothing: "ACT gains about 7 and DVE 2 against PE's 166: hidden by PE at 27.9 of 27.9, taken as 0." A full PE says that its partners kept up, not that they had room for 7 us: the kernel before, as full, lost 1.6 to two table loads put into chunk 2. The step also looked for ACT's room in the whole run; what counted where those loads stood was the stretch in which exponential, r_mul and gate follow one another on a PSUM ring of two banks. The price of the cover when it is gone was not worked out. The runs give some of it: two of the loads 1.6 to 1.8; 10.7 us of work on three engines in chunk 2, 2.9. The new order of chunks 2 to 5, which the prediction did not walk through at all, was fitted to its choices (undoing them cost another 3.4) but had no slack to give.

**First gate: right in kind, too early by 0.8, and not in every execution.** 28.33 where 27.5 was forecast, a gain of 1.42 for 2.25. The waits were taken rightly. From 8.10 to the end of xn_out.1.1 at 28.19 DVE stood idle 0.94, where 0.9 was forecast; its 37 steps were busy 19.15 where 18.5 was summed (columns as before, then a w_tot that the sum had at 0.1):

```profile
8.10:28.19 20.09, 16.47 (x200) 10.80 (x197) 19.15 (x37) 15.24 (x36) 14.96 (x20) 1.00 1.09 212
```
```profile
21.83 0.91 DVE L447 TENSOR_TENSOR wcol<-er,half_of 128x16 f32<-128x16 f32 x1 [0.22 <-ACT er L251]
```

The sum was short although rk_tr, its dearest step, cost half of what was taken:

```profile
27.04 0.68 DVE L496 COPY rkT<-ps_qv 128x1024 bf16<-128x1024 bf16 x1
```

The next DVE step starts 0.60 later, not 1.2. With the long half rate at the start, 30.06, there is no gain at all. By the Trainium skill, VectorE: DVE Perf Modes (The perf-mode tier table), up to twice the rate was allowed, and the trace agrees with it, against my reading from xn_out.

**Weights: too dear.** 0.98 of waiting for 2.3; the net is -0.1 instead of +1.2, and o_mm waits for no weight, as forecast.

**PE work: right.** A narrow triple takes 0.33 (52.12 - 51.79), as taken, and PE is full from 50 to 80.

**The last FFN's cover** was taken as 0 with a bound of 1.1: its gates waited 0.64 (174.34), and those of the FFN ahead of it 0.44, which the prediction had not looked at.

**Rivals.** C priced the right mechanism, PE tied to DVE and ACT, at the wrong place: groups 1 and 2 ran at full rate, chunk 2's entry and the FFNs behind them did not, and its 203.1 was too low. D's outcome, no earlier first gate, stands in four of fourteen traces, but by PE's half rate in the first 10 us and not by DVE's waits for loads; B's better start was outweighed; E's clock did not fall at the first gates, and how long the half rate at the start lasts was not asked. The range ended at 203.2 because none of them let the order of chunks 2 to 5 count.

**What stays open.** Of the 7 us some 3 follow the load on the partners up to and in chunk 3; two table loads alone give back 1.8, and whether these are part of the 3 is not shown. From 4.0 (less ACT) to 4.8 us remain in every run with work left out in chunks 2 to 5. Rows put 0.86 + 0.32 of it at chunk 2's entry (behind the table load of 44.75, and in all fourteen traces) and some 1.1 at the gains ahead of the last two FFNs, less the better start, which in some executions is 1.7 worse; no run took these away together, and no version was found that beats the kernel before.
